# A head's 144 coarse queries as 64 + 64 + 48 rows instead of 72 + 72, in the attention of batches 2 and 3

## The chip, the cores and the metric

The kernel runs on one core of a Trainium2 chip. The metric is the device time of one execution in microseconds (us); lower is better. The time before is the median of three runs.

## The reference

An attention layer feeds two feed-forward layers. The attention has a coarse part (queries, keys and values averaged over groups of four positions: 576 positions become 144) and a local part (each position sees its neighbours at a distance below 4); their outputs are added.

```python
# B, H, S, D = 4, 8, 576, 64; factor = 4; Sd = 144
out_d = sm_attn(q_d, k_d, v_d)               # softmax over 144 coarse keys
out_up = np.repeat(out_d, factor, axis=2)
...
out_local = np.matmul(attn, v)               # |i - j| < 4
x = (out_up + out_local) as (2304 tokens, 512)
h = x @ moe_w_in;  x = (h * sigmoid(1.702 h)) @ moe_w_out       # 512 -> 2048 -> 512
h = x @ moe2_w_in; out = elu(h) @ moe2_w_out                    # 512 -> 2048 -> 512
```

All is float32. The weights arrive as 64-bit floats and are converted in the kernel.

## The kernel before

The work on attention is cut into units: one batch and two heads (a head pair), held on partitions 0 to 63 and 64 to 127. Batch 0 and 1 are computed in an opening whose order is written out by hand, up to about 160 us. Batches 2 and 3 make eight units of the class `Packed`, which are also in the set `turned`. These eight, between about 160 and 335 us, are what the change touches. Their pieces are put by a queue between the matmuls of the first feed-forward layer: the function `step1` runs a layer step (12 matmuls "h", line 1300, or 12 matmuls "y", line 1367) and calls `attend()` between them, which takes the next piece off the queue. TensorE runs in exactly the written order. A unit has four pieces.

- `all_scores` (lines 991 to 1016): four coarse score products (line 1004; for each head 72 and 72 queries as the stationary operand, 144 coarse keys moving), then 20 local score products of 64 x 64 (line 1026, `qk_products`). Then on VectorE the row maxima (line 1011), their scaling (`down_scale`, line 627), the masks (line 1041) and the local maxima; then on ScalarE the exponentials of the coarse rows (`exp_down`, line 668). Each float32 product is two instructions of TensorE in the trace, so line 1004 has 8 and line 1026 has 40 for each unit.
- `turn` of the unit after it, on VectorE only.
- `turned_over`: the rows of probabilities, already divided by their sums (`weigh_down`, line 703), are transposed on TensorE: one local pair of windows (line 1068), eight pieces of the coarse rows of 72 x 72 (`pdt_piece`, line 725), four more local pairs (line 1068). ScalarE copies the coarse result to `pdT` (line 733). A float32 transpose is one instruction.
- `pv`: products with the values (line 1092 coarse, line 1127 local), and the sum of both.

`turned_over` of a unit comes after `all_scores` of the unit that follows it, so its operands have been ready for long.

Two PSUM banks belong to the attention (tag "s"). Two more (tag "h") hold the results of the "h" steps in turn; the coarse scores of the first head, and later the transposed rows of the second, borrow one of them (`more`).

[...] An operand that starts at partition 64 is written in the code by a slice such as `r = slice(64 * j, 64 * j + 64)`, and the rows of the result by the slice of the output.

Of the kernel before, what the change touches and what calls it, by code (L numbers as in the profile page):

```python
# [8 lines left out]
F32 = mybir.dt.float32  # L9
# [5 lines left out]
AF = mybir.ActivationFunctionType  # L15
ALU = mybir.AluOpType
AX = mybir.AxisListType

P = 128
D = 64  # L20
S = 576
SD = 144
HALF = 72
# [105 lines left out]
def kernel(  # L129
# [20 lines left out]
    nc = tc.nc  # L150
# [9 lines left out]
    hpool = ctx.enter_context(tc.tile_pool(name="hpool", bufs=2, space=PSUM))  # L160
# [6 lines left out]
    ident = cpool.tile([P, P], F32, tag="ident", name="ident")  # L167
# [4 lines left out]
    for half in range(2):  # L172
        rows = slice(64 * half, 64 * half + 64)
        for a, e, lo in ((0, 1, -3), (1, 5, 0), (5, 6, 3)):
            m = mask[rows, a:e, :]
            for step, base, mult in ((1, -lo, -1), (-1, lo + 6, 1)):
                nc.gpsimd.affine_select(
                    out=m, in_=m, pattern=[[0, e - a], [step, KW]], compare_op=ALU.is_ge, fill=NEG,
# [218 lines left out]
    class Unit:  # L397
# [158 lines left out]
        def qk_products(self, a, e):  # L556
            if a == self.w0:
                self.sl = self.t([P, self.nwin, KW], "sl", bufs=2)
                self.nm = self.dn_from.nm if self in late else self.t([P, NWIN], "nm", bufs=4)
            ps = self.ps([P, e - a, KW], f"qk{a}")  # L560
            m0 = 0 if a == 0 else 6 - (e - a) if e == NWIN else 1
            by_pe = self in early or self in late
            if by_pe:
                nc.tensor.matmul(
                    out=ps.rearrange("p a b -> p (a b)"), lhsT=identb,
                    rhs=mask[:, m0:m0 + e - a].rearrange("p a b -> p (a b)"),
                    start=True, stop=False, skip_group_check=True,
                )
            for w in range(a, e):
                ks = win_start(w)  # L570
                for j in range(2):
                    r = slice(64 * j, 64 * j + 64)
                    nc.tensor.matmul(  # L573
                        out=ps[r, w - a, :], lhsT=self.qkT[0][r, 64 * w:64 * w + 64],
                        rhs=self.qkT[1][r, ks:ks + KW], start=not by_pe, stop=True, skip_group_check=True,
                    )
            if by_pe:
                self.scores = ps
            return ps
# [80 lines left out]
                    func=AF.Exp, bias=self.nm[:, w:w + 1], accum_out=self.sums()[:, w:w + 1],  # L660
                )

        def down_part(self, i):
            return self.psd[i // 2][:, i % 2, :]

        def exp_down(self):
            for i in range(4):
                nc.scalar.activation(
                    out=self.pd[:, i, :], in_=self.down_part(i), func=AF.Exp, bias=self.nmd[:, i:i + 1],
                    scale=self.scale_down(), accum_out=self.sums()[:HALF, self.nslot + i:self.nslot + i + 1],  # L670
                )

# [34 lines left out]
        def weigh_down(self):  # L707
            self.weigh_part(self.pd, self.sums()[:HALF, self.nslot:self.nslot + 4])
# [6 lines left out]
                deferred.pop(0)()  # L715
            self.pdt_copy(j, self.pdt_piece(j))

        def pdt_piece(self, j, ps=None):
            if j == 0:
                self.pdT = self.t([HALF, 4, SD], "pdT")  # L720
            if ps is None:
                ps = self.ps([HALF, 2, SD], f"pdt{j}")
            for kc in range(2):
                for c in range(2):
                    nc.tensor.transpose(  # L725
                        out=ps[:, kc, c * HALF:(c + 1) * HALF],
                        in_=self.pd[:, 2 * j + c, kc * HALF:(kc + 1) * HALF],
                        identity=ident[:HALF, :HALF],
                    )
            return ps  # L730
# [212 lines left out]
    class Packed(Unit):  # L943
# [42 lines left out]
        def more(self, nm):  # L986

            full = hpool.tile([P, 512], F32, tag="h", name=f"{nm}_{self.n}")
            return full[:HALF, :2 * SD].rearrange("p (c k) -> p c k", c=2)

        def all_scores(self):


            n = NPAIR * 64
            banks = [self.ps([P, n + SD], f"qk{j}") for j in range(2)]
            self.nmd = self.t([HALF, 4], "nmd", bufs=4)
            self.pd = self.t([HALF, 4, SD], "pd", bufs=2)
            more = self.more("qkd")
            parts = [more[:, 0], more[:, 1], banks[0][:HALF, n:], banks[1][:HALF, n:]]
            self.psd = [parts[:2], parts[2:]]  # L1000
            for i, ps in enumerate(parts):
                j, c = i // 2, i % 2
                r = slice(64 * j, 64 * j + 64)
                nc.tensor.matmul(
                    out=ps, lhsT=self.qkd[0][r, c * HALF:(c + 1) * HALF], rhs=self.qkd[1][r, :],
                    start=True, stop=True, skip_group_check=True,
                )
            local = self.qk_products([ps[:, :n].rearrange("p (a b) -> p a b", b=64) for ps in banks])
            nmd = self.nmd
            for to, ps in ((nmd[:, :2], more), (nmd[:, 2:3], parts[2]), (nmd[:, 3:], parts[3])):  # L1010
                nc.vector.tensor_reduce(out=to, in_=ps, axis=AX.X, op=ALU.max, negate=True)
            self.down_scale()
            for j, ps in enumerate(local):
                self.qk_mask(j, ps)
            self.qk_largest()
            self.exps()

        def qk_products(self, ps=None):
            self.sl = self.t([P, NSLOT, 64], "sl", bufs=2)
# [29 lines left out]

        def qk_largest(self):  # L1050
            nc.vector.tensor_reduce(out=self.nm, in_=self.sl, axis=AX.X, op=ALU.max, negate=True)

        def down_part(self, i):
            return self.psd[i // 2][i % 2] if self in turned else super().down_part(i)

        def exps(self):
            self.exp_down()
# [137 lines left out]
    turned = rest[NHP:]  # L1195
# [212 lines left out]
    kd, f = spare.pop(0)  # L1408
# [263 lines left out]
    for s in range(LAG, len(steps2) + LAG):  # L1672
        if s < len(steps2):
            hidden2(s)
        f = steps2[s - LAG][1]
# [34 lines left out]
```

## Time and profile before

| | us |
|---|---|
| median of the runs (lowest, highest) | 911.7 (911.44, 912.12) |
| the profiled execution, its own time | 911.03 |
| its span, first to last instruction | 909.2 |

The profiled execution has 1.83 us outside its span, and lies 0.67 us below the median. In the views below a chain row gives the start, the length and the piece of work that ended last; a group "qk" or "qkd" names the PSUM tile that is written. In shapes such as "64*72 64x144" the stationary operand comes first (rows * columns), then the moving one. PE is TensorE, PEld its weight load, DVE VectorE, ACT ScalarE.

### The profile page before, as it was taken

The numbers are of one execution on the slowest core, as the hardware profiler recorded it, in microseconds if no ns is written. First come the engines' busy times: TensorE is split into PE (matmuls) and PEld (weight loads), VectorE is DVE, ScalarE is ACT, GpSimd is POOL, SyncE is SP. The second block draws the span as 40 slices with busy tenths as digits, with TensorE's granted clock in tenths as the row PEclk, the third lists the DMA queues.
The fourth block names the chain that finished last, engine by engine and source line by source line (L and its number), as shares of the span: only waits on it lengthen the run. The fifth ranks groups of instructions, "written<-read, shape, count | busy, mean of one in ns | idle before, by whom it ended". The sixth has DMA issues, their size and how long they took to land.

```text
span 909.2 us, 14831 instructions
## 1 busy us (share of the span) xinstructions
PE 900.2 (99%) x5816; PEld 748.4 (82%) x5816; DVE 461.5 (51%) x896; ACT 441.7 (49%) x1094; POOL 63.1 (7%) x126
## 2 busy tenths in 40 slices
PE   8999999999999999999999999999999999999998
PEld 5789878788888888888899888888888888888897
DVE  5999986765667532322247785632223223322232
ACT  6898874444445422422255776643334334333343
POOL 4502322011111100000000000000000000000000
PEclk9999999999999999999999999999999999999999
DMA  9688743432233000100069830010001000100000
GB/s 175 185 243 238 198 130 71 99 58 56 54 72 90 23 15 1 47 1 0 1 216 377 287 93 1 0 47 1 1 15 67 1 1 12 47 1 1 14 33 24
DMA packets 113862, 68.06 MB, mean 75 GB/s; under 512 B 81152, under 2 KB 103424, under 8 KB 113792
## 3 DMA queue, kind: packets, MB, share of 16 engines
q1 hardware_dynamic: 111280, 66.39, 26.1%
q10 hardware_dynamic: 2512, 0.72, 0.4%
q8 instruction: 46, 0.75, 0.4%
q14 instruction: 24, 0.20, 0.1%
HBM read 57.65 MB, written 9.44 MB: 74 GB/s over the span
## 4 chain that ended last, share of the span: by engine, by line
PE 92%; DVE 4%; DMA 2%; SPq 1%; ACT 1%; issue 0%; DVEq 0%; ACTq 0%
PE h L1504 22%; PE o L1556 22%; PE h L1300 18%; PE y L1367 17%; PE y_both L1367 3%; PE h_both L1300 2%; DMA rawq<-in_q_dram 1%; PE pv L1127 1%; PE pdt L725 1%; PE qk L1026 1%; PE pt L520 1%; DMA wst1i<-in_moe_w_in_dram 1%; PE ptr L1068 1%; PE qkd L615 1%; PE pv L1092 1%; PE qk L573 1%
## 5 line engine op out<-in xcount | busy, mean ns | idle before, releaser
L1556 PE MATMUL o<-whl2o,g2h 128*128 128x512 f32 x576 | 178.5, 391 | 0.0
L1367 PE MATMUL y<-g1h,whl1o 128*128 128x512 f32 (+1 forms) x512 | 151.2, 366 | 1.6 <-ACT ye_both L1381 1.6
L1514 DVE SCALAR_TENSOR_TENSOR g<-e,h 128x512 f32<-128x512 f32 (+1 forms) x80 | 50.7, 634 | 195.4 <-ACT e L1512 195.3
L1300 PE MATMUL h<-xh,whl1i 128*128 128x512 f32 (+1 forms) x640 | 144.8, 351 | 0.1
L1556 PEld LDWEIGHTS o<-whl2o,g2h 128*128 128x128 f32 x576 | 107.1, 188 | 22.3 <-DVE whl2o L245 0.3
L1511 ACT ACTIVATE e<-h 128x512 f32<-128x512 f32 (+1 forms) x80 | 44.5, 556 | 158.0 <-PE h L1504 157.6
L1300 PEld LDWEIGHTS h<-xh,whl1i 128*128 128x128 f32 x640 | 105.9, 189 | 16.7 <-issue 0.6
L1556 PE MATMUL o<-whl2o,g2l 128*128 128x512 f32 x288 | 112.4, 390 | 0.0
L1367 PEld LDWEIGHTS y<-g1h,whl1o 128*128 128x128 f32 x512 | 92.5, 189 | 17.1 <-ACT ye_both L1381 2.1
L1313 DVE SCALAR_TENSOR_TENSOR g<-g,h 128x512 f32<-128x512 f32 x64 | 43.8, 684 | 123.1 <-ACT g L1309 123.1
L1504 PE MATMUL h<-x2h,whl2i 128*128 128x512 f32 x352 | 94.8, 391 | 0.0
L1309 ACT ACTIVATE g<-h 128x512 f32<-128x512 f32 x64 | 38.2, 596 | 114.3 <-PE h L1300 113.9
L1367 PE MATMUL y<-g1l,whl1o 128*128 128x512 f32 (+1 forms) x256 | 92.9, 363 | 0.0
L1504 PEld LDWEIGHTS h<-x2h,whl2i 128*128 128x128 f32 x352 | 66.0, 188 | 14.2
L1300 PE MATMUL h<-xl,whl1i 128*128 128x512 f32 (+1 forms) x320 | 73.0, 347 | 0.0
L1521 DVE TENSOR_TENSOR g2l<-g,g2h 128x512 fp32r<-128x512 f32 (+1 forms) x80 | 51.0, 638 | 37.9 <-PE o L1556 22.4
L1519 ACT ACTIVATE g2h<-g 128x512 fp32r<-128x512 f32 (+1 forms) x80 | 47.1, 589 | 44.4 <-DVE g L1514 44.4
L1556 PEld LDWEIGHTS o<-whl2o,g2l 128*128 128x128 f32 x288 | 54.1, 188 | 11.7
L1504 PE MATMUL h<-x,whl2i 128*128 128x512 f32 (+1 forms) x336 | 63.0, 337 | 0.0
L1300 PEld LDWEIGHTS h<-xl,whl1i 128*128 128x128 f32 x320 | 54.1, 189 | 7.7
L1504 PEld LDWEIGHTS h<-x,whl2i 128*128 128x128 f32 x336 | 53.6, 189 | 7.9
L1326 DVE TENSOR_TENSOR g1l<-g,g1h 128x512 fp32r<-128x512 f32 x64 | 44.4, 695 | 27.1 <-ACT g1h L1319 26.3
(170 smaller groups left out, 1290.7 us busy)
## 6 DMA issues: line engine op xcount, KB each, us to landing
wst1i<-in_moe_w_in_dram SPq DMA_DIRECT2D x16, 512.0 KB
wst1o<-in_moe_w_out_dram SPq DMA_DIRECT2D x16, 512.0 KB
wst2o<-in_moe_w_out_dram SPq DMA_DIRECT2D x16, 512.0 KB
wst2i<-in_moe_w_in_dram SPq DMA_DIRECT2D x16, 512.0 KB
vr<-in_v_dram SPq DMA_DIRECT2D x32, 144.0 KB
out_dram<-ot SPq DMA_DIRECT2D x17, 256.0 KB
y<-ydram SPq DMA_DIRECT2D x16, 256.0 KB
ydram<-ye SPq DMA_DIRECT2D x14, 256.0 KB
```

The source lines that it names most:

```text
L520: nc.tensor.transpose(out=pt[:, j, :], in_=raw[:, 3 * i + j].rearrange("p h d -> p (h d)"), identity=ident[:96, :96],)
L1300: nc.tensor.matmul(out=hps[blk, fs][:, i, :], lhsT=w_in(1, f, c, wp), rhs=columns(xp, c), start=(n == 0), stop=(n >= len(todo) - nf), skip ...
L1309: return nc.scalar.activation(out=g, in_=hps[blk, fs], func=AF.Tanh, scale=0.851)
L1313: return nc.vector.scalar_tensor_tensor(out=g, in0=g, scalar=1.0, in1=ph, op0=ALU.add, op1=ALU.mult)
L1326: return nc.vector.tensor_tensor(out=gl, in0=g, in1=gh.bitcast(F32), op=ALU.subtract)
L1367: nc.tensor.matmul(out=sums(m), lhsT=w_out(1, f, wp)[:, m, :], rhs=gp[:, i, :], start=(opens and n == 0 and m % per == 0), stop=(last and ...
L1504: nc.tensor.matmul(out=ph[:, :n], lhsT=w_in(2, f, c, wp), rhs=xp[c][:, :n], start=(i == 0), stop=(i == 3 * NK - 1),)
L1511: nc.scalar.activation(out=e[:, :n], in_=ph[:, :n], func=AF.Relu, scale=-1.0)
L1514: urgent["dve"] = nc.vector.scalar_tensor_tensor(out=g[:, :n], in0=e[:, :n], scalar=-1.0, in1=ph[:, :n], op0=ALU.add, op1=ALU.max)
L1519: nc.scalar.activation(out=gh[:, :n], in_=g[:, :n], func=AF.Copy)
L1521: return lambda: nc.vector.tensor_tensor(out=gl[:, :n], in0=g[:, :n], in1=gh[:, :n].bitcast(F32), op=ALU.subtract)
L1556: nc.tensor.matmul(out=ops[bi][i], lhsT=gp[:, i * P:(i + 1) * P], rhs=wo[wp], start=(f == 0 and m == 0), stop=(f == NF - 1 and m == 2),)
```

## The change

For the eight `turned` units the 144 coarse queries of head j are computed as queries 0 to 63, 64 to 127 and 96 to 143. The first two make a tile of 128 rows, one for each head, in that head's bank of local scores. The third has 48 queries, of which the last 16 (128 to 143) are used: the "tail". Both tails share the borrowed bank, head 0 in rows 32 to 47, head 1 in rows 96 to 111. The six products are written with the heads alternating, each with a result in one half of the partitions. Maxima, scaling, exponentials and weighing go over four pieces (two of 128 rows, two of 16) instead of tiles of 72 rows. In the transposes each head has for each half of the keys one piece of 128 rows by 72 and one of 16 rows by 72, written in turns, in place of two of 72 by 72. The number of transposes stays eight. Batch 1, which is `Packed` too but not in `turned`, keeps its form.

```diff
-            more = self.more("qkd")
-            parts = [more[:, 0], more[:, 1], banks[0][:HALF, n:], banks[1][:HALF, n:]]
-            self.psd = [parts[:2], parts[2:]]
-            for i, ps in enumerate(parts):
-                j, c = i // 2, i % 2
+            more = hpool.tile([P, 512], F32, tag="h", name=f"qkd_{self.n}")[:, :SD]
+            self.psd = [ps[:, n:] for ps in banks] + [more]
+            for j, at, q0, m in ((0, 0, 0, 64), (1, 2, 96, 48), (0, 0, 64, 64), (1, 1, 0, 64), (0, 2, 96, 48), (1, 1, 64, 64)):
                 r = slice(64 * j, 64 * j + 64)
+                c = 64 * j if at == 2 else q0
                 nc.tensor.matmul(
-                    out=ps, lhsT=self.qkd[0][r, c * HALF:(c + 1) * HALF], rhs=self.qkd[1][r, :],
+                    out=self.psd[at][c:c + m, :], lhsT=self.qkd[0][r, q0:q0 + m], rhs=self.qkd[1][r, :],
                     start=True, stop=True, skip_group_check=True,
                 )
...
-            nmd = self.nmd
-            for to, ps in ((nmd[:, :2], more), (nmd[:, 2:3], parts[2]), (nmd[:, 3:], parts[3])):
-                nc.vector.tensor_reduce(out=to, in_=ps, axis=AX.X, op=ALU.max, negate=True)
-            self.down_scale()
+            for out, ps in self.down_parts(self.nmd):
+                nc.vector.tensor_reduce(out=out, in_=ps, axis=AX.X, op=ALU.max, negate=True)
+                nc.vector.tensor_scalar(out=out, in0=out, scalar1=self.scale_down(), scalar2=None, op0=ALU.mult)
...
+        def down_parts(self, *of):
+            for i in range(4):
+                at, rows = (i, slice(0, P)) if i < 2 else (2, self.tail(i - 2))
+                yield (*(t[rows, at:at + 1] for t in of), self.psd[at][rows])
+        def weigh_down(self):
...
+            self.weigh_part(self.pd[:, :2], sums[:, :2])
+            for j in range(2):
+                self.weigh_part(self.pd[self.tail(j), 2:3], sums[self.tail(j), 2:3])
...
+        def pdt_piece(self, j, ps=None):
...
+            for kc in range(2):
+                k = slice(kc * HALF, kc * HALF + HALF)
+                rows = self.tail(j)
+                nc.tensor.transpose(out=ps[:, kc, :P], in_=self.pd[:, j, k], identity=ident)
+                nc.tensor.transpose(out=ps[:, kc, P:], in_=self.pd[rows, 2, k], identity=ident[rows, rows])
```

`tail(j)` is `slice(64 * j + 32, 64 * j + 48)`.

## Rows read from the trace of the kernel before

**Rows 1.** The profile page: busy time by engine, and the chain's share by engine.

```profile
PE 900.2 (99%) x5816; PEld 748.4 (82%) x5816; DVE 461.5 (51%) x896; ACT 441.7 (49%) x1094; POOL 63.1 (7%) x126
...
PE 92%; DVE 4%; DMA 2%; SPq 1%; ACT 1%; issue 0%; DVEq 0%; ACTq 0%
```

**Rows 2.** Windows: one unit's period; PE, PEld, DVE, ACT, POOL busy, clock, DMA.

```profile
199.90:220.70 20.80, 20.80 (x182) 16.72 (x181) 12.78 (x29) 9.27 (x38) 2.73 (x6) 1.00 0.30 59
```

**Rows 3.** The chain that ended last, one unit's period: start, length, work.

```profile
200.08 0.27 PE qkd L1004
200.35 0.01 PE qk L1004
200.36 0.11 PE qkd L1004
...
200.73 0.74 PE qk L1026 x40
201.47 2.96 PE h L1300 x12
204.43 2.72 PE y L1367 x12
207.15 2.72 PE h L1300 x12
209.88 0.11 PE ptr L1068
209.99 0.25 PE ptr L725 x4
210.24 0.25 PE pdt L725 x4
210.49 0.44 PE ptr L1068 x4
210.93 2.76 PE y L1367 x12
...
216.41 0.64 PE pv L1092 x8
217.05 0.84 PE pv L1127 x40
```

**Rows 4.** TensorE in order of time, start of one unit's scores.

```profile
200.01 0.34 PE L1004 MATMUL qkd<-kd,qd 64*72 64x144 f32 x1
200.02 0.34 PE L1004 MATMUL qk<-kd,qd 64*72 64x144 f32 x1
200.19 0.28 PE L1004 MATMUL qkd<-kd,qd 64*72 64x144 f32 x1
```

**Rows 5.** Groups by line and shape, TensorE, 160 to 340 us: busy us, mean ns.

```profile
L1068 PE MATMUL ptr<-ident,sl 128*128 128x128 f32 x40 | 7.0, 272 | 0.0
...
L725 PE MATMUL ptr<-ident,pd 72*72 72x72 f32 x32 | 3.3, 226 | 0.0
```

**Rows 6.** The chain again, at the seventh unit's scores, where TensorE waits.

```profile
283.22 0.60 ACT g L1309
...
283.85 0.70 DVE g L1313
...
284.59 3.01 PE h L1300 x12
```

**Rows 7.** Groups by line and shape, VectorE, 160 to 340 us.

```profile
L703 DVE TENSOR_TENSOR pd<-pd,sumset 72x576 f32<-72x576 f32 x8 | 5.9, 743 | 0.1
...
L1011 DVE TENSOR_REDUCE nmd<-qk 72x1 f32<-72x144 f32 x16 | 4.1, 298 | 2.2 <-PE qk L1026 2.2
...
L1011 DVE TENSOR_REDUCE nmd<-qkd 72x2 f32<-72x288 f32 x8 | 3.6, 453 | 8.6 <-PE qkd L1004 8.6
...
L627 DVE TENSOR_SCALAR nmd<-nmd 72x4 f32<-72x4 f32 x8 | 1.5, 187 | 0.0
```

**Rows 8.** ScalarE in order of time: the last coarse exponential of that unit.

```profile
203.75 0.37 ACT L668 ACTIVATE pd<-qk,nmd 72x144 f32<-72x144 f32 x1
```

More of the change, by code (lines that the diff above doesn't have):

```diff
@@ L661, in exp_windows @@
                 )
-        def down_part(self, i):
-            return self.psd[i // 2][:, i % 2, :]
         def exp_down(self):
@@ L668, in exp_down @@
                 nc.scalar.activation(
-                    out=self.pd[:, i, :], in_=self.down_part(i), func=AF.Exp, bias=self.nmd[:, i:i + 1],
+                    out=self.pd[:, i, :], in_=self.psd[i // 2][:, i % 2, :], func=AF.Exp, bias=self.nmd[:, i:i + 1],
                     scale=self.scale_down(), accum_out=self.sums()[:HALF, self.nslot + i:self.nslot + i + 1],
@@ L716, in pdt, with pdt_piece @@
             self.pdt_copy(j, self.pdt_piece(j))
-        def pdt_piece(self, j, ps=None):
+        def pdt_piece(self, j):
             if j == 0:
                 self.pdT = self.t([HALF, 4, SD], "pdT")
-            if ps is None:
-                ps = self.ps([HALF, 2, SD], f"pdt{j}")
+            ps = self.ps([HALF, 2, SD], f"pdt{j}")
             for kc in range(2):
@@ L989, in more, with tail @@
             return full[:HALF, :2 * SD].rearrange("p (c k) -> p c k", c=2)
+        def tail(self, j):
+            return slice(64 * j + 32, 64 * j + 48)
         def all_scores(self):
@@ L995, in all_scores @@
             banks = [self.ps([P, n + SD], f"qk{j}") for j in range(2)]
-            self.nmd = self.t([HALF, 4], "nmd", bufs=4)
-            self.pd = self.t([HALF, 4, SD], "pd", bufs=2)
-            more = self.more("qkd")
-            parts = [more[:, 0], more[:, 1], banks[0][:HALF, n:], banks[1][:HALF, n:]]
-            self.psd = [parts[:2], parts[2:]]
-            for i, ps in enumerate(parts):
-                j, c = i // 2, i % 2
+            self.nmd = self.t([P, 4], "nmd", bufs=4)
+            self.pd = self.t([P, 4, SD], "pd", bufs=2)
+            more = hpool.tile([P, 512], F32, tag="h", name=f"qkd_{self.n}")[:, :SD]
+            self.psd = [ps[:, n:] for ps in banks] + [more]
+            for j, at, q0, m in ((0, 0, 0, 64), (1, 2, 96, 48), (0, 0, 64, 64), (1, 1, 0, 64), (0, 2, 96, 48), (1, 1, 64, 64)):
                 r = slice(64 * j, 64 * j + 64)
+                c = 64 * j if at == 2 else q0
                 nc.tensor.matmul(
-                    out=ps, lhsT=self.qkd[0][r, c * HALF:(c + 1) * HALF], rhs=self.qkd[1][r, :],
+                    out=self.psd[at][c:c + m, :], lhsT=self.qkd[0][r, q0:q0 + m], rhs=self.qkd[1][r, :],
                     start=True, stop=True, skip_group_check=True,
@@ L1016, in all_scores, with exp_down @@
             self.exps()
+        def down_parts(self, *of):
[3 more added lines that the diff above has]
+        def weigh_down(self):
+            if self not in turned:
+                super().weigh_down()
+                return
+            sums = self.sums()[:, self.nslot:self.nslot + 3]
+            self.weigh_part(self.pd[:, :2], sums[:, :2])
+            for j in range(2):
+                self.weigh_part(self.pd[self.tail(j), 2:3], sums[self.tail(j), 2:3])
+        def exp_down(self):
+            if self not in turned:
+                super().exp_down()
+                return
+            for pd, bias, total, ps in self.down_parts(self.pd, self.nmd, self.sums()[:, self.nslot:]):
+                nc.scalar.activation(
+                    out=pd[:, 0], in_=ps, func=AF.Exp, bias=bias, scale=self.scale_down(), accum_out=total
+                )
+        def pdt_piece(self, j, ps=None):
+            if self not in turned:
+                return super().pdt_piece(j)
+            if j == 0:
+                self.pdT = self.t([HALF, 4, SD], "pdT")
+            for kc in range(2):
[3 more added lines that the diff above has]
+                nc.tensor.transpose(out=ps[:, kc, P:], in_=self.pd[rows, 2, k], identity=ident[rows, rows])
+            return ps
         def qk_products(self, ps=None):
@@ L1051, in qk_largest @@
             nc.vector.tensor_reduce(out=self.nm, in_=self.sl, axis=AX.X, op=ALU.max, negate=True)
-        def down_part(self, i):
-            return self.psd[i // 2][i % 2] if self in turned else super().down_part(i)
         def exps(self):
```

## The prediction

> **What bounds the kernel now.** I read the page first. TensorE is busy for 99% of the span, and 92% of the chain that ended last is TensorE's [rows 1]. [...] Then the chain through such a period. The reader is to see that it holds nothing but TensorE's work, piece behind piece, so that each row's length is what that piece costs the kernel: a feed-forward step takes 2.72 us, and the four attention pieces stand between such steps [rows 3]. The change must therefore be costed on TensorE, in what it adds to or takes from these rows; VectorE and ScalarE come into it only if they become late.
>
> The same rows show a second thing. A step of 12 matmuls takes 2.72 us, but 2.96 us right behind the local scores: 0.24 us more on the way back from operands of 64 rows and 64 columns to the full array. The first pair of coarse products takes 0.28 us (0.27 and 0.01), each later pair 0.12 us (0.01 and 0.11): 0.16 us more on the way in. The whole-array transposes of line 1068 and line 725 pay nothing of the kind on the way in (0.11 us for the first one, as for each of the four later ones, 0.44 / 4), and the step after them takes 2.76 us, 0.04 more [rows 3]. So what costs is not a small operand or a transpose. It is the passage between instructions that use the whole array and instructions that use a part of it.
>
> **Coarse scores.** Now four products for each unit, 64 rows by 72 columns. The two heads already run side by side: the tiles "qkd" (head 0) and "qk" (head 1) start 0.01 us apart, the next pass 0.18 us later [rows 4]. So alternating the heads gives nothing by itself. Cost now: 0.16 in, four pairs of passes at 0.12 = 0.48, together 0.64; then the 40 local instructions in 0.74 [rows 3]. A pass of 144 columns takes 0.12 us, so one of 64 columns takes 0.12 x 64 / 144 = 0.053. Forty of them two at a time would be 1.07 us, more than the 0.74 shown; four at a time they are 0.53. So four quarters of the array do work at once, and 0.74 - 0.53 = 0.21 us is a passage too, from 64 x 72 to 64 x 64.
>
> After the change the coarse products have at most 64 columns, the form of the local ones, and that passage should go. The six products fill quarters in the order (head 0, lower), (1, upper), (0, upper), (1, lower), (0, lower), (1, upper). No quarter has more than two products, each of two passes: 4 x 0.12 = 0.48, as now. New sum: 0.16 + 0.48 + 0.53 = 1.17 against 1.38, a gain of 0.2 us. Bounds: if only two of the six run at once, they take 6 x 0.12 = 0.72 and the gain is 0.21 - 0.24, about nothing; if the passage was worth as much as the one from line 1092 to line 1127 (0.84 us for 40 instructions of about 58 columns, 10 x 0.049 = 0.49 of streaming, 0.35 over) it is 0.35. I take 0.2, the difference of this place itself. In the seventh unit it is lost: there TensorE waits after the scores for ScalarE and VectorE (L1309, then L1313) before the next step can have its bank [rows 6]. So the gain is 7 x 0.2 = 1.4 us, bounds 0 and 2.5.
>
> **Transposes of the coarse rows.** Now eight of 72 x 72 in 0.50 us, 0.062 each; 128 columns take 0.11 [rows 3]. After the change: four with 128 moving columns, four with 16. Streaming: 4 x 0.11, and a tail between 0.014 us (16 columns at (0.11 - 0.062) / 56 a column) and 0.062 (a 72-column one). With 0.03 that is 0.56, +0.06 us; bounds 0 and +0.19.
>
> The form counts for more. The wide piece has 128 rows, the whole height of the array. The tail has 16 rows that start at partition 32 or 96, and its result 72 columns. Operands of 64 rows that start at partition 64 run as a part of the array of their own [rows 4], so I take a tail to be a part too. The four wide ones and the four tails are written in turns, and line 1068 follows the last tail: four passages in and four out for each unit, where there is none now. By the rows 4 x (0.16 + 0.24) = 1.60 us, with the streaming +1.66.
>
> A second way to the price goes by durations. Behind a passage an instruction ends its whole length after its predecessor, where otherwise it ends only its streaming time after: the first coarse pair ends 0.28 us on. A transpose lasts 0.272 us with 128 columns and 0.226 with 72 [rows 5], so a tail lasts about 0.226 - 0.05 = 0.18. The block of L1068, eight pieces and L1068 x4 then is 0.11 + 0.11 + 4 x 0.18 + 3 x 0.27 + 0.27 + 3 x 0.11 = 2.35 us, against 1.05 now: +1.30. The weight load that the passage out leaves bare (0.24 - 0.16 = 0.08, four times) would make it 1.62. I take 1.5, between the two. No row here has an operand of 16 or 32 rows, so the price is bounded by nothing below and by 8 x 0.35 = 2.8 us above (the dearest passage, line 1127).
>
> [...]
>
> **VectorE and ScalarE.** Maxima and scaling now take 0.45 + 2 x 0.30 + 0.19 = 1.24 us; then four maxima of 144 elements at 0.30 and four scalings at 0.19, 1.96: +0.7 us. Weighing the coarse rows takes 0.74 for 576 elements a row; then 288 and twice 144 elements, which is the same 576 and two fixed parts more (0.30 - 0.15 each, as 0.453 for 288 against 0.298 for 144 gives): about +0.3 [rows 7]. The four exponentials keep their 144 elements. VectorE has 8 us of idle time in a period [rows 2], so +1.0 is hidden. What waits for it: the borrowed bank, which now is read by the last two exponentials in place of the first two, and the step that starts at 207.15 needs it. The last exponential starts at 203.75 [rows 8]. One microsecond later leaves 2 us. Should that cover be gone, TensorE would wait for what is over, under 1 us a unit. I cost it at nothing. No DMA and no queue is touched.
>
> **Sum.** 8 x 1.5 - 1.4 = +10.6 us, against the profiled execution 911.03 + 10.6 = 921.6, and against the median, which lies 0.67 higher, 922.3. TensorE has no slack in which this could vanish: all eight transposing blocks lie in chain stretches like the one shown [rows 3].
>
> **The rivals.** (a) The tails cost no passage: a 16-row piece shares the array with the full height as the 72-row piece does now. Then +0.06 x 8 - 1.4 = -0.9, 910.8 us: no change by measurement, for which I take 0.2%, 1.8 us, as the bound. For it: no 16-row operand stands in the trace. Against it: the passage from the full array to 64 rows is paid with all columns in use (72 of them), so splitting rows alone costs. (b) As (a), and the coarse scores gain 0.35 a unit: +0.5 - 2.5 = -2.0, 909.7 us, faster. It is the other side, and its place is the entry of line 1026. It decides only if the eight passages together cost under 0.03 us a unit. (c) The passages are cheaper, since a tail of 16 columns has little to drain: half price, 0.75 a unit, +6.0 - 1.4 = 4.6, 916.3. Against it: the second way above already lets the tail be short. (d) They are dearer, 0.35 each: 8 x 2.86 - 1.4 = +21.5, 933 us. For it there is line 1127 alone.
>
> [...]
>
> **How the numbers follow.** The forecast (a price between 1.2 and 1.9 us a unit: 919.9 to 925.5) has 0.62, (c) 0.15, (a) 0.10, (b) 0.05, (d) and what lies toward it 0.08. Slower: 0.62 + 0.15 + 0.08 = 0.85; within 0.2%: 0.10; faster: 0.05. The range goes from 914, the lower side of (c), to 928, a third of the way from the forecast's top to (d). It leaves out (a), (b) and most of (d), 2 in 10.
>
> **What would show it.** In the chain a period grows from 20.80 to about 22.1 us. The block between the "h" step and the "y" step (1.05 us) becomes about 2.5, with each tail and each wide piece 0.2 to 0.3 us apart, at a TensorE that has no wait there. Line 1026 falls from 0.74 to about 0.53 while line 1004 keeps about 0.64. The step behind the local scores keeps its 2.96. Wrong would be: transposes at 0.11 and 0.03 apart, as in (a); or a wait in front of an "h" step for ScalarE's exponentials, which would be the borrowed bank.

## The result and the profile after

The changed kernel takes 919.79 us (median of 6 runs, 918.11 to 921.04) against 911.68 before: a ratio of 1.0086, 95% interval 1.0075 to 1.0097, or +8.1 us. The forecast was 922.3. These lines of the profile page of the changed kernel answer to [rows 1]: TensorE is still what is busy.

```profile
span 919.3 us, 14941 instructions
...
PE 908.6 (99%) x5848; PEld 752.1 (82%) x5848; DVE 470.4 (51%) x944; ACT 447.2 (49%) x1094; POOL 63.1 (7%) x126
```

The chain through one unit's period, as in [rows 3]. Line 1026 has become 1060, line 1068 is 1099, line 725 is 1048 (128 rows) and 1049 (the tails); "h" is 1331, "y" 1398.

```profile
204.11 0.28 PE qk L1004 x3
204.49 0.12 PE qk L1004 x4
204.68 0.64 PE qk L1060 x34
205.32 2.95 PE h L1331 x12
208.27 2.72 PE y L1398 x12
...
213.72 0.11 PE ptr L1099
213.83 0.11 PE ptr L1048
213.94 0.13 PE ptr L1049
214.07 0.23 PE ptr L1048
214.30 0.14 PE ptr L1049
214.44 0.23 PE pdt L1048
214.67 0.13 PE pdt L1049
214.81 0.23 PE pdt L1048
215.04 0.13 PE pdt L1049
215.18 0.59 PE ptr L1099 x4
215.76 2.76 PE y L1398 x12
...
225.67 0.28 PE qk L1004 x3
```

The first wide transpose ends 0.11 us behind the one ahead of it, as any of 128 columns did before. Each tail then takes 0.13 to 0.14, and each wide one behind a tail 0.23 in place of 0.11. The weight loads show what differs: that of the first wide piece starts 0.10 us ahead of its transpose (213.56 and 213.66), those of the tail and the wide piece behind it start with theirs (213.86 and 213.87, then 214.00 and 214.00). The last tail is paid for in the local transposes, 0.59 for four against 0.44 in [rows 3]. The block of transposes takes 215.76 - 213.72 = 2.04 us against 1.05: +0.99 for each of eight units, 7.9 us. The scores take 205.32 - 204.11 = 1.21 against 201.47 - 200.08 = 1.39: -0.18. The period is 21.56 us; before, it was 20.76, from 200.08 to the next unit's 220.84. TensorE waits nowhere in it.

One thing does not show in a period like this. TensorE's waits from 160 to 350 us (us in total, how many, the longest), and the granted clock in two stretches, in the same execution (columns as in [rows 2]):

```profile
PE y L1398 <- ACT ye_both L1412: 2.1, 1, 2.1
PE h L1331 <- DVE g L1344: 0.3, 1, 0.3
...
181.00:184.00 3.00, 3.00 (x55) 2.77 (x55) 1.61 (x8) 0.89 (x4) 0.00 (x0) 0.50 0.90 182
184.00:190.00 6.00, 6.00 (x27) 4.93 (x27) 3.84 (x10) 5.12 (x26) 0.00 (x0) 0.96 0.21 32
```

In the first row TensorE's "y" step waits for ScalarE to empty a bank. This wait, at about 178 us, was 1.6 us long before and is 2.1 now. (The second row, 0.3 us, is the seventh unit, where the gain on the scores is lost.) Behind the wait of 2.1 us the clock was granted at 0.50 from 181 to 184 us and at 0.96 from 184 to 190. The second unit's scores and the "h" step behind them then ran from 181.01 to 186.71, 5.70 us; in a second trace of the same kernel (after_again), where the clock stayed at 1.00, from 180.00 to 184.17, 4.17 us. So the fall of the clock cost 1.5 us in that execution. The spans of the two traces differ by more, 919.3 against 916.7 us: the first unit's scores already start 1.0 us later in the first (165.89 against 164.88), in an opening that the two have in common.

### The profile page after: what moved, and what is told of

Same layout as the page of the kernel before. It is cut to its first block, busy times and chain, and to the rows that moved or that the text cites. A ratio compares the mean times of both kernels' runs of the same rounds, so it can differ in the third digit from the quotient of the medians.

```text
span 919.3 us, 14941 instructions
## 1 busy us (share of the span) xinstructions
PE 908.6 (99%) x5848; PEld 752.1 (82%) x5848; DVE 470.4 (51%) x944; ACT 447.2 (49%) x1094; POOL 63.1 (7%) x126
## 4 chain that ended last, share of the span: by engine, by line
PE 87%; DVE 10%; issue 1%; ACT 1%; DMA 1%; SPq 0%; DVEq 0%; ACTq 0%
PE h L1535 22%; PE o L1587 21%; PE y L1398 17%; PE h L1331 16%; PE y_both L1398 3%; PE h_both L1331 2%; PE pv L1158 1%; DVE ww1o L234 1%; PE ptr L1099 1%; DMA rawq<-in_q_dram 1%; DVE nmd L622 1%; DVE whl1o L245 1%; DVE ww1i L234 1%; DVE g1l L1357 1%; DVE g L1344 1%
```

## The experiments

Theory: the time goes to the passages of TensorE between the whole array and the 16-row tails. Rivals: the 128-column transposes and the new tiles themselves, VectorE's added work, or the wait and the clock at 178 us.

**One passage for each unit (a_grouped).** All four wide transposes, then all four tails.

```diff
             for j in range(2):
                 self.pdt_piece(j, down[j])          # now the two wide ones only
+            for j in range(2):
+                self.pdt_tails(j, down[j])          # the two tails of head j
             first = self.pt_first()
```

> The changed kernel with the four wide transposes of a unit written first and the four tails behind them, so that the tails are entered and left once for each unit instead of four times; nothing else differs. If the passages are the cost: in the changed kernel the block of transposes takes 2.04 us against 1.05 before; with one passage in and out it should take 0.11 + 4 x 0.11 + about 0.13 + 3 x 0.03 + 0.59 = 1.36, so 8 x 0.68 = 5.4 us less than the changed kernel's 919.8: about 914.4. If the cost is the 128-column transposes, VectorE's added work or the low clock behind the wait at 178 us: about 919 to 920, as the changed kernel.

Measured: 913.25 us, ratio to the kernel before 1.0014 (1.0006 to 1.0023). The chain through its block:

```profile
211.99 0.11 PE ptr L1103
212.10 0.22 PE ptr L1047 x2
212.32 0.22 PE pdt L1047 x2
212.54 0.14 PE ptr L1054
212.67 0.01 PE pdt L1054
212.68 0.03 PE ptr L1054
212.71 0.01 PE pdt L1054
212.72 0.59 PE ptr L1103 x4
```

The first tail costs 0.14 us; the three behind it, of the same form and two of them of the other head, 0.05 together. The tails are not dear, their turns with the wide pieces are: the same block takes 1.31 us in this order and 2.04 in the other, 8 x 0.73 = 5.8 us. This trace has the wait of 2.1 us at 178 us and a granted clock of 0.83 from 180 to 190 us, as the changed kernel's first trace has. So VectorE's work, the wait and the clock are not what cost the 8 us.

**Passages alone, in the kernel before (d_passages).** A 16-row transpose ahead of each pair of 72-row ones.

```diff
             for kc in range(2):
+                if self in turned:
+                    nc.tensor.transpose(
+                        out=ps[:, kc, :16], in_=self.pd[32:48, 2 * j, kc * HALF:(kc + 1) * HALF],
+                        identity=ident[32:48, 32:48],
+                    )
                 for c in range(2):
```

> The kernel before, with four transposes of 16 rows (partitions 32 to 47) by 72 added for each of the eight units, one ahead of each pair of 72 x 72 transposes, their results written over by the transposes behind them. Scores, VectorE and ScalarE are as before. If the passages are the cost: four in and four out for each unit, about 0.25 us each pair as in the changed kernel (a tail ends 0.14 us after the wide piece, the piece behind it 0.12 us later than without), 8 x 1.0 to 1.1 = 8 to 9 us: 920 to 921. If the wide transposes, VectorE or the clock are the cost: only the streaming, 32 x 0.014 to 0.06 = 0.5 to 2 us: 912 to 914.

Measured: 919.98 us, ratio 1.0084 (1.0071 to 1.0098): nearly all of what the change cost, with scores, VectorE and ScalarE as before, the wait at 1.6 us and the clock at 1.00. Its block in the chain (line 725 is the added piece, 730 the 72-row ones):

```profile
212.49 0.11 PE ptr L1073
212.59 0.14 PE ptr L725
212.73 0.25 PE ptr L730 x2
212.98 0.14 PE ptr L725
213.11 0.25 PE ptr L730 x2
```

Two 72-row transposes take 0.25 behind such a piece; four took 0.25 in [rows 3].

**No 16-row operand (b_full, c_half).** The third product of a head holds 64 queries, 80 to 143, so that its tile is full; the 16 rows wanted are taken out by a product of the whole height. In c_half the transposed rows lie by key half, and one product serves both heads.

```diff
-((0, 0, 0, 64), (1, 2, 96, 48), (0, 0, 64, 64), (1, 1, 0, 64), (0, 2, 96, 48), (1, 1, 64, 64))
+((0, 0, 0, 64), (1, 2, 80, 64), (0, 0, 64, 64), (1, 1, 0, 64), (0, 2, 80, 64), (1, 1, 64, 64))
...
-                nc.tensor.transpose(out=ps[:, kc, P:], in_=self.pd[rows, 2, k], identity=ident[rows, rows])
+            nc.tensor.matmul(          # c_half; b_full: rhs=ident[:, rows], once for each head
+                out=ps[:, :, P:], lhsT=self.pd[:, 2, k], rhs=ident.rearrange("p (j q) -> p j q", j=2)[:, :, 48:],
+                start=True, stop=True, skip_group_check=True,
+            )
```

> The changed kernel with the third piece of a head holding queries 80 to 143 (64 of them) in place of 96 to 143, so that all 128 rows of that tile are filled; maxima, scaling, exponentials and weighing go over three tiles of 128 rows, and the tails are taken out by plain float32 products of the whole height, 128 rows by 72 with 16 columns of the identity (two instructions each), in place of 16-row transposes. No operand of 16 rows is left, so no passage in the transposes. If the passages are the cost: block of transposes 0.11 + 4 x 0.11 + 8 x 0.03 to 0.06 + 0.44 = 1.2 to 1.5 us, and the gain of 0.18 us a unit on the scores stays: 911 to 914 us. If the wide transposes or the third tile are the cost: 918 to 920.

> As the full-height variant, but the transposed rows lie by key half in their banks, so that one product takes out the tails of both heads (32 columns): 4 wide transposes and 2 products for each unit. If the passages are the cost: block 0.11 + 0.44 + 4 x 0.03 to 0.06 + 0.44 = 1.1 to 1.2 us, as before the change or 0.15 above, with 0.18 us a unit won on the scores: 910.5 to 912.5, at or a little below the kernel before. With less work on VectorE and one exponential fewer on ScalarE for each unit, TensorE's wait at 178 us should be shorter than the 1.64 us of before. If the cost lies elsewhere: 918 to 920.

Measured: b_full 912.65 (1.0006, 0.9998 to 1.0015), c_half 911.68 (0.9996, 0.9988 to 1.0005), both with the kernel before at 911.96. The chain through c_half's block:

```profile
209.59 0.11 PE ptr L1105
209.69 0.22 PE ptr L1045 x2
209.91 0.09 PE ptr L1046 x2
210.01 0.23 PE pdt L1045 x2
210.23 0.09 PE pdt L1046 x2
210.33 0.47 PE ptr L1105 x4
210.80 2.77 PE y L1404 x12
```

The wide transposes take 0.11 us each (0.22 or 0.23 for two), also behind a tail product. The block takes 1.21 us, 0.16 more than before, and the scores 1.22, 0.17 less: the two cancel, and c_half is the kernel before within the measurement. The 128-column transposes are cleared. TensorE's wait at 178 us is 1.6 us in both, so it did not become shorter, as was expected of c_half. In b_full the tail products and the wide transposes still take turns:

```profile
209.07 0.08 PE ptr L1047 x2
209.15 0.13 PE ptr L1046
```

A wide transpose (line 1046) takes 0.13 us behind such a product, where it took 0.23 behind a 16-row tail. So it is not the alternation of two kinds of piece that costs, but that one of them is a 16-row piece.

**The turns of the heads (g_order).** c_half with head 0's three products written first.

```diff
-((0, 0, 0, 64), (1, 2, 80, 64), (0, 0, 64, 64), (1, 1, 0, 64), (0, 2, 80, 64), (1, 1, 64, 64))
+((0, 0, 0, 64), (0, 0, 64, 64), (0, 2, 80, 64), (1, 1, 0, 64), (1, 1, 64, 64), (1, 2, 80, 64))
```

> The variant with the tails taken out by key half, with the six coarse products of a unit written head by head (three of head 0, then three of head 1) in place of in turns; the rest is the same. If TensorE lets the two heads run side by side however they are written, as it did in the kernel before: scores and local products in 1.22 us as in that variant, about 911.7 us. If the turns are needed: head 1 starts only when head 0 is done, up to 0.36 us more a unit, 2.5 to 3 us: 914.5.

Measured: 912.05 us (1.0003, 0.9994 to 1.0011); scores and local products take 1.24 us in its chain (200.49 to 201.73) against 1.22. The turns of the heads did nothing for the time. [rows 4] had shown the same: head 1's first product is written third there and starts 0.01 us behind head 0's first, ahead of head 0's second at 200.31. So between the two heads the starts do not follow the written order, which the description of the kernel takes to be exact.

**VectorE's share (e_vector, after_again).** First its work cut as in the changed kernel, in the kernel before; and the changed kernel once more.

```diff
-            for to, ps in ((nmd[:, :2], more), (nmd[:, 2:3], parts[2]), (nmd[:, 3:], parts[3])):
-                nc.vector.tensor_reduce(out=to, in_=ps, axis=AX.X, op=ALU.max, negate=True)
-            self.down_scale()
+            for i, ps in enumerate(parts):
+                to = self.nmd[:, i:i + 1]
+                nc.vector.tensor_reduce(out=to, in_=ps, axis=AX.X, op=ALU.max, negate=True)
+                nc.vector.tensor_scalar(out=to, in0=to, scalar1=self.scale_down(), scalar2=None, op0=ALU.mult)
...
+            for a, n in ((0, 2), (2, 1), (3, 1)):     # weigh_down
```

> The kernel before with VectorE's work for the eight units cut as in the changed kernel, and nothing else: four maxima of 144 elements, each with a scaling of its own behind it, in place of three maxima and one scaling, and the weighing of the coarse rows in three pieces in place of one. TensorE's and ScalarE's instructions are as before. If VectorE's added work lengthens TensorE's wait at 178 us (1.6 us before, 2.1 in the changed kernel) and the wait then lets the clock fall to its lower level: the wait is about 2.1 us, the granted clock of 180 to 190 us is below 1.00, and the time is 0.5 to 2 us above before, 912.5 to 914. If the added work is hidden everywhere and wait and clock come from TensorE's own changes: 911.5 to 912.3, wait 1.6, clock 1.00.

> The changed kernel once more, beside the others. If the wait at 178 us and the low clock behind it belong to its order on VectorE: a wait of about 2.1 us again and a granted clock below 1.00 between 180 and 190 us in most executions, 918 to 921 us. If they were an accident of the one execution shown: wait 1.6, clock 1.00, and the time near 918.

Measured: e_vector 911.43 us (0.9998, 0.9989 to 1.0006), wait 1.6, clock 1.00. This refutes the theory that the number of VectorE's pieces makes the longer wait. The changed kernel again: 919.05 (1.0083, 1.0069 to 1.0096), wait 2.1 again, clock 1.00 this time. So the wait belongs to the kernel, and the fall of the clock only to some of its executions: the mean granted clock of the whole execution is 0.998 or lower in 5 of its 11 (4 of the first 6, and 1 of 5 here, where most were expected). The first maxima and scalings of the first unit on VectorE, in order of time, e_vector and then the changed kernel:

```profile
165.91 0.52 DVE L1011 TENSOR_REDUCE nmd<-qkd 72x1 f32<-72x144 f32 x2 [2.02 <-PE qkd L1004]
166.35 0.26 DVE L1012 TENSOR_SCALAR nmd<-nmd 72x1 f32<-72x1 f32 x2
```

```profile
165.55 0.65 DVE L1010 TENSOR_REDUCE nmd<-qkd 16x1 f32<-16x144 f32 x2 [2.01 <-PE qkd L1004]
166.23 0.32 DVE L1011 TENSOR_SCALAR nmd<-nmd 16x1 f32<-16x1 f32 x2
```

Two maxima of 144 elements take 0.52 us together when both start at partition 0, and 0.65 when one starts at 32 and the other at 96; the scalings follow 0.44 us after the first start in the one, 0.68 in the other. From the first maximum to the local maxima that follow it is 2.37 us in e_vector and 2.76 in the changed kernel, and the weighing takes 0.81 and 1.10: 0.68 us more in all, for as many pieces and as many elements a row. That made a new theory: pieces with different start partitions do not overlap.

**Start partitions (i_twostarts, h_onestart).** c_half with as many VectorE instructions as the changed kernel, in i_twostarts over rows 0 to 63 and 64 to 127 of the third tile, in h_onestart always from partition 0. For the weighing h_onestart cuts the third tile by columns, 72 and 72, so a row has 288 + 72 + 72 elements there and 288 + 144 + 144 in i_twostarts.

```diff
+            for at, rows in ((2, slice(0, 64)), (2, slice(64, P)), (0, slice(0, P)), (1, slice(0, P))):
+                out = self.nmd[rows, at:at + 1]          # h_onestart: rows 0 to P in all four
+                nc.vector.tensor_reduce(out=out, in_=self.psd[at][rows], axis=AX.X, op=ALU.max, negate=True)
+                nc.vector.tensor_scalar(out=out, in0=out, scalar1=self.scale_down(), scalar2=None, op0=ALU.mult)
```

> The variant with the tails taken out by key half, with VectorE's work on the third tile cut into two pieces that start at partitions 0 and 64 (maxima, scalings and weighing), so that VectorE has the same number and order of instructions as in the changed kernel. If pieces at different start partitions don't overlap on VectorE (in the changed kernel two maxima at partitions 32 and 96 took 0.65 us, in the kernel with VectorE's work cut at partition 0 alone 0.52), the wait at 178 us is about 2.0 to 2.1 us and the way from the first unit's scores to the second's is 15.0 us, against 14.27 in that variant. If the number of pieces alone counted, e_vector would have shown it; if the 16 rows of the tails counted, the wait stays at 1.6 and the way at 14.3.

> The same variant with as many VectorE instructions, but every one over 128 rows from partition 0 (the third tile's maximum and scaling are done twice; its weighing is cut by columns, 72 and 72). If the start partition is what counts: wait 1.6 to 1.8 us, way from the first unit's scores to the second's 14.3 to 14.5 us. If the number of instructions counts: wait 2.0 to 2.1, way 15.0, as in the kernel with two starts.

Measured: i_twostarts 913.12 us (1.0018, 1.0007 to 1.0029), h_onestart 911.69 (1.0009, 0.9999 to 1.0018), beside the kernel before at 910.76. TensorE's waits, i_twostarts first:

```profile
PE y L1406 <- ACT ye_both L1420: 2.0, 1, 2.0
```

```profile
PE y L1406 <- ACT ye_both L1420: 1.7, 1, 1.7
```

The way to the second unit's scores, which the expectations name, is 14.45 us in h_onestart and 15.39 in i_twostarts, but behind the wait the clock fell in the latter's trace (0.83 from 180 to 190 us). So I compare the way from the first unit's scores to the end of the wait (the end of ScalarE's copy in the chain). It is 13.24 us in c_half, 13.43 in h_onestart and in e_vector, 14.01 in i_twostarts and 14.11 in both traces of the changed kernel. The weighing in the chains of i_twostarts, then of h_onestart:

```profile
175.42 0.58 DVE pd L700 x2
176.02 0.31 DVE pd L700
```

```profile
176.00 0.65 DVE pd L700 x3
```

Of the 0.77 us that i_twostarts adds to c_half, h_onestart's pieces explain 0.19. Of the other 0.58, an estimated 0.15 is the longer rows of the weighing (two pieces of 144 elements in place of two of 72; the changed kernel's pieces took 0.449 us for 288 elements a row and 0.302 for 144, so 72 elements are worth about 0.07), which leaves about 0.43 to the start partitions. And since the pieces of i_twostarts have 64 rows, it is not the 16 rows of the tails that count: its way from the first maximum to the local maxima is 2.76 us, as in the changed kernel.

The times do not show this by themselves. The executions with a mean clock of 0.999 or 1.000 are alike, 911.41 to 911.97 us in i_twostarts (four) and 910.69 to 912.70 in h_onestart (nine); the medians differ with the clock, which was lower in six of ten executions of the one and in one of ten of the other. The verdict rests on one trace of each, and no run shows by itself why pieces with different start partitions take longer.

## Why the forecast came out

**What bounds the kernel.** Right. TensorE's chain took the cost of the transposes piece by piece, and none of it vanished. VectorE and ScalarE did become late at one place, at 178 us, which the prediction allowed for in words and not in the sum.

**Coarse scores.** Right: 0.18 us a unit for a forecast 0.2. Line 1060 keeps 0.64 us where the 0.53 was named, and line 1004 ends earlier (0.57 from 204.11 to 204.68): the two overlap, and only the sum of 1.21 against the named 1.17 can be compared. That the passage between them is gone is read from the order of the starts on TensorE. Before, and then in the changed kernel (its first unit):

```profile
200.45 0.28 PE L1004 MATMUL qk<-kd,qd 64*72 64x144 f32 x1
200.66 0.81 PE L1026 MATMUL qk<-kT,qT 64*64 64x64 f32 x40
```

```profile
166.12 0.28 PE L1004 MATMUL qkd<-kd,qd 64*48 64x144 f32 x1
166.13 0.27 PE L1060 MATMUL qk<-kT,qT 64*64 64x64 f32 x2
...
166.24 0.28 PE L1004 MATMUL qkd<-kd,qd 64*48 64x144 f32 x1
```

Before, the local products began 0.21 us behind the start of the last coarse one; now they begin among the coarse ones. No run takes the 64-column form back by itself, so this is read and not tested. The step behind keeps 2.95. That the turns give nothing by themselves is shown by g_order.

**Transposes.** The mechanism was right, and shown from three sides: fewer passages (a_grouped), passages alone (d_passages), none (b_full, c_half). The size was too large: 1.5 us a unit was taken, 0.99 is what it is, and that lies below the forecast's own bracket of 1.2 to 1.9. The term that was off is the passage, 0.40 for one in and one out. Behind a wide transpose a tail takes 0.13 to 0.14, behind another tail about 0.02, so the way in costs 0.12; the way out costs 0.12 to the next wide one and 0.15 to the local ones. That is 0.24 to 0.27 for the two, where products in and feed-forward steps out had shown 0.16 and 0.24. The second way, by whole durations, missed as well: a wide transpose behind a tail lasts 0.303 us but ends only 0.23 after it. So the price of a passage is not the same for each kind of instruction, and the rows used were of score products and feed-forward steps, not of transposes. Every tail here has 16 rows and starts at partition 32 or 96. No run has a 16-row piece at partition 0, so whether the height or the start makes the passage is not separated.

That a 16-row tail runs as a part of the array of its own, so that all eight passages are paid, was the author's estimate from the products of 64 rows. The runs agree with it: going from the whole array to a tail or back cost 0.12 to 0.15 us each time, while in a_grouped a tail behind a tail took 0.01 to 0.03 us, though they lie in different rows.

**VectorE and ScalarE.** Costed at nothing, and wrong by 0.7 us, with up to 1.5 more in an execution where the clock fell. The step read one period, in which VectorE is idle for 8 us, and took it for the whole stage. Ahead of the wait at 178 us VectorE has no idle time to hide in: it was busy for 5.88 of the 6 us from 172 to 178 before the change. And it is not the number of the added instructions that made it (e_vector adds as many, and 0.01 us): their start partitions made most of it, by i_twostarts (an estimated 0.43 of the 0.77 us that it adds to c_half). The borrowed bank, of which the step spoke, never made TensorE wait.

**The sum.** Forecast +10.6; measured +8.1. From the traces: 8 x 0.99 = 7.9; -0.18 for six units, -1.1 (in the seventh the gain is lost in the wait of [rows 6], as named, and the first is in the next term); +0.7 for the way to the end of the wait at 178 us (14.11 against 13.42 before): +7.5. The trace with the clock at 1.00 throughout has a span of 916.7 against 909.2, +7.5. The rest of the median goes with the clock: the six of the changed kernel's eleven executions with a mean clock of 0.999 or 1.000 took 918.11 to 919.12 us, the other five 919.36 to 921.04. In the traces the clock fell behind three of the four waits of 2.0 us or more and behind none of the seven of 1.6 or 1.7. Over all executions the difference is one of frequency: the mean clock is 0.998 or lower in 16 of 32 executions of the kernels whose traces have the longer wait, and in 22 of 126 of those with the shorter one, 15 of them of the kernel before. Where in the span it fell is known from the traces alone; that the longer wait lets it fall is an observation, not shown by itself.

**Rivals.** (a) and (b) fell with d_passages, (d) with the first trace. The price, 0.99, lies between the forecast's 1.5 and (c)'s 0.75, and nearer to (c)'s. That a tail has little to drain, the reason given for (c), was the author's guess, which no run shows. That the time still came out at the lower edge of the forecast's own bracket (919.79 against 919.9) is partly luck: two costs that the prediction put at nothing, 0.7 us at the wait and about 0.6 us with the clock, made up for part of the 4.1 us (8 x 0.51) by which the transposes had been priced too high.

What was not tried: score products of 64 columns whose results still lie in tiles of 72 rows. If the gain comes from the form of the products alone, that would keep it and leave the transposes as they were; no run shows it.

## What to carry to other kernels

Look at the forms of neighbouring TensorE instructions before looking at their sizes: here a change from whole-array operands to 16-row ones and back cost 0.24 to 0.27 us, and a 72-row transpose 0.06. How many such changes there are is set by the order in which the instructions are written. So put pieces of one form together (1.31 us for the block in place of 2.04), or compute some rows that are thrown away to keep one form (1.21). When a layout is changed to spare one engine a passage, follow the new rows through every consumer: here 0.18 us was won in the scores and 0.99 paid in the transposes. And a stage's idle time must be read ahead of each wait, not in the mean of a period.

## What was not expected of the hardware

The two row halves of TensorE ran side by side even when all products of one were written ahead of those of the other (g_order, 1.24 us against 1.22). Two maxima of 144 elements on VectorE at different start partitions took 0.13 us more than two at the same one (0.65 against 0.52). A tail behind another tail added 0.01 to 0.03 us, also where it lies in other rows of the array (a_grouped), so what cost here is the change of form and not the change of place.
